# A linear-attention layer with a rational feed-forward on one core: a new order table for the same tasks

## The chip, the cores and the metric

The kernel runs on one core of one Trainium2 chip. The metric is the device time of one execution in microseconds (us). The engines are named as in the profile: PE is TensorE (matmuls; PEld its weight loads), DVE is VectorE, ACT is ScalarE, POOL is GpSimd, SP is SyncE, which only issues transfers here.

## The reference

Two layers follow one another. The first is a linear attention with a decay `w` and a bonus `u` for each head; the second is a feed-forward layer whose activation is a quotient of polynomials. The batch is 4, with 8 heads, 768 positions and 48 elements a head, so the feed-forward sees 3072 rows of 384.

```
for t in range(S):
    cur = einsum('bhd,bhe->bhde', u * k[t], v[t])
    y[t] = einsum('bhd,bhde->bhe', r[t], state + cur)
    state = w * state + einsum('bhd,bhe->bhde', k[t], v[t])
x = y as (3072, 384)
h = x @ w_in                                     # 384 -> 2048
P = a[0] + a[1]*h + a[2]*h**2 + a[3]*h**3
Q = 1 + abs(b[0])*abs(h) + abs(b[1])*h**2
out = (P / (Q + 1e-6)) @ w_out                   # 2048 -> 384
```

## The kernel before

**The attention** works on 24 blocks of 128 positions, two to a token tile of 256. A task of the order table is written as a name, the block or slice, a letter for the engine (P TensorE, D VectorE, A ScalarE, G GpSimd, S SyncE) and a named place for its result. For block n: `Lr`, `Lk`, `Lv` load r, k and v, `LV` brings v into the operand of `y` (a load, or a copy of 64x192 on a compute engine); `sr` and `sk` scale r and k with powers of w; `ba`, `bb`, `bs`, `bv` make the bonus (product, product with u, sum, product with v); `tr` and `tk` transpose r and k on TensorE and `tre`, `tke` copy the result out of its bank; `a` multiplies r and k in tiles of 64x64, `ae` masks it; `kv` makes the change of the state, `kve` adds it and `ca` scales the state; `y` is the output of the block, `ye` adds the bonus; `x` transposes y, `xh` and `xl` store it as a high and a low part (an fp32 number as two).

**The feed-forward** works on 12 token tiles. The 2048 hidden columns are 16 pieces of 128, and a slice s is (as a rule) four of them for one token tile; there are 50 slices. `f1.s.j` makes 128 hidden columns with 9 matmuls of 128x256 (three chunks of the 384, each high by high, high by low, low by high). Its result is in one of two `h` buffers of PSUM. On the slice's 128x1024 elements follow `z`, `q`, `t`, `ln`, `ex` on ScalarE and `u3`, `hi`, `p`, `d`, `lo` on VectorE. `hi` and `lo` are the two parts of the activation; `lo` is the last to read `h` and so frees the buffer for `f1` of slice s+2. `f2.s.half` multiplies them by `w_out`, 12 matmuls of 128x384 for each half of the tokens. `os` brings the sums of a visit to SBUF or adds them there, `od` issues the transfer of the output.

**The weights** come as 28 pieces that are loaded (`cl`) and turned into two fp32 parts by `c0`, `cu`, `ch` on ScalarE, `c2`, `c3` on VectorE and `cr`, `co` on GpSimd (`co` now and then on VectorE). They are spread over the first 150 us. At the very start `pow` makes the powers of w by a scan, `inv` their reciprocals, `sq` is a chain of small instructions on roots of the coefficients, and `turn`, `tab` and `wp` bring the powers into their places over TensorE.

`warm.n` issues n filler matmuls of ones with ones, whose results nobody reads. They only keep TensorE at work while it has nothing else.

**What sets the order.** The table `ORDER` is a string of tasks and is worked off under a manual schedule: each engine's instructions stand in its queue in the order in which the table names its tasks, and wait there for what they need. Nothing is decided at run time. The table was written by a planner outside of the kernel. Buffers are of two kinds: places that the table names (`ta`, `pa`, `h`, `m`), and pools that go around in a fixed turn (`os` with 6 buffers, `dt` with 2, `ldv` with 3, `xt` with 3).

Of the kernel before, what the change touches and what calls it, by code (L numbers as in the profile page):

```python
# [52 lines left out]
tr.0Ppa1 tab.1A c3.6D Lk.1S tre.0.1A warm.8P wpPpa0 tre.0.0A sr.1G warm.2P tr.1Ph1 tre.1.0A tre.1.1A cl.2S Lv.0S sk.2D ba.2Dm0
bb.2D bs.2D sk.0G warm.12P tk.0Ph0 ba.0Gm1 bb.0G kv.2Ppa1 cl.5S sk.1D bv.2D tke.0A a.0Ph1 ba.1Gm2 c0.2A kve.2.1A w128A kve.2.0A
Lr.3S ae.0.0D c2.2Dpa0 Lv.1S cu.2A pad.2G ae.0.1D bb.1G warm.3P kv.0Ph0 Lk.3S kve.0.1A cr.6Gta0 cl.12S tk.1Ppa1 tke.1A bs.0D bv.0G
c3.2D cr.2Gta1 kve.0.0A cl.1S warm.38P kv.1Ph1 c0.5A cu.5A LV.0.1.0A sk.3G sr.3G c2.5Dpa1 ba.3Gm3 bb.3G bs.1D bv.1G LV.0.0.1D
c3.5D LV.0.1.1A a.1Ppa0 ae.1.0D tk.2Ph0 ae.1.1D LV.0.0.0A y.0Ppa1 warm.3P tr.2Ppa0 kve.1.1A c0.12A kve.1.0A c2.12Dh1 ye.0D cl.0S
cl.26S tke.2A c0.1A c2.1Dh0 tre.2.0A Lr.4S Lk.5S ca.0.0G cl.4S warm.10P kv.3Ppa1 tre.2.1A Lk.4S cu.12A c3.12D warm.4P x.0Ph1 ch.2A
a.2Ppa0 Lv.4S xh.0A bs.3D kve.3.0A c3.1D y.1Ph0 kve.3.1A c0.26A xl.0D tr.3Ppa1 cr.12Gta2 cu.1A ae.2.0D ch.12A ae.2.1D warm.6P
y.2Ppa0 tre.3.0A c2.26Dh1 Lv.5S ye.1D x.1Ph0 c0.0A c3.26D warm.1P tk.3Ph1 sr.4G ca.0.1G tre.3.1A xh.1A cl.3S tke.3A ye.2D warm.3P  # L60
x.2Ppa1 xh.2A cu.0A c2.0Dpa0 co.12G xl.1D c3.0D ca.1.0G cr.1Gta3 ch.1A warm.12P a.3Ph1 sk.5D ca.1.1G ae.3.0D tr.4Ph0 cu.26A sk.4G
ba.4Gm1 warm.5P kv.4Ppa0 cl.11S cr.0Gta4 tre.4.0A c0.4A tre.4.1A warm.12P kv.5Ph0 xl.2D co.2G c0.3A cl.9S ae.3.1D cu.3A cl.20S
Lr.5S cu.4A c2.4Dpa1 ch.6A tk.4Ph1 tke.4A kve.4.0D kve.4.1D c3.4D kve.5.1D ch.0A bv.3D c2.3Dpa0 warm.17P a.4Ppa1 tk.5Ph1 co.1D
cu.9A cu.11A c0.11A cr.5Gta5 cl.15S c3.3D cu.20A cl.10S cl.14S kve.5.0D c0.9A warm.15P y.3Ppa0 co.0G f1.0.0Ph0 f1.0.1P tke.5A
# [20 lines left out]
bb.8G cr.17Gta0 ch.17A co.17G f1.7.2P cu.18A cr.18Gta3 LV.4.1.1S os.4.0D LV.4.1.0S bs.7D bv.7G u3.6D ln.6A ex.6A kve.7.0D kve.7.1D
c0.24A f2.5.0P f2.5.1P c2.19Dpa0 c3.19D hi.6Dta0 p.6D tk.8Ppa1 cu.19A cr.19Gta1 tke.8A cu.24A ch.19A co.19G y.6Ppa0 ye.6D tr.8Ppa1
ch.18A f1.7.3P tre.8.1A y.7Ppa0 ca.7.1G tre.8.0A a.8Ppa1 z.7Ata2 d.6D lo.6Dta1 ca.5.0G sk.9G f1.8.0Ph0 t.7Ata5 ye.7D x.6Ppa0 q.7A
co.18G ae.8.0D u3.7D ae.8.1D f1.8.1P f1.8.2P f1.8.3P os.5.0D sr.9G LV.4.0.0S xh.6A xl.6D ln.7A ex.7A os.5.1D f2.6.0P x.7Ppa1
ch.27A cu.25A cr.25Gta6 ch.25A c2.24Dpa0 c3.24D Lk.10S hi.7Dta3 p.7D tr.9Ppa0 tre.9.1A f2.6.1P ca.6.0G xh.7A ca.7.0G co.25G d.7D
tre.9.0A xl.7D kv.8Ppa0 Lk.11S z.8Ata0 lo.7Dta1 kv.9Ppa1 kve.9.0D kve.9.1D cr.24Gta6 ch.24A t.8Ata2 u3.8D f1.9.0Ph1 f1.9.1P  # L90
kve.8.0D sk.10G ba.10Gm2 bb.10G q.8A ln.8A ex.8A co.27D tk.9Ppa1 tke.9A ba.9Gm0 f1.9.2P f1.9.3P z.9Ata5 kve.8.1D bs.8D co.24G
f2.7.0P hi.8Dta4 ca.6.1G Lk.12S sk.12G a.9Ppa1 y.8Ppa0 Lv.10S p.8D d.8D lo.8Dta6 bb.9G bv.8G t.9Ata0 u3.9D Lr.12S f2.7.1P os.7.1D
# [4 lines left out]
f1.11.0Ph1 f1.11.1P os.9.1D ae.10.1D x.9Ph0 xh.9A xl.9D ae.10.0D f1.11.2P kve.10.0D sr.12G os.9.0D ca.9.1G f1.11.3P f1.12.0Ph0
t.11Ata0 f1.12.1P z.11Ata2 q.11A kv.11Ppa1 bs.10D bv.10G Lv.13S kve.10.1D f1.12.2P ba.12Gm1 u3.11D ln.11A bb.12G kve.11.0D
kve.11.1D kv.12Ppa0 kve.12.0D kve.12.1D ba.13Gm0 y.10Ppa1 ye.10D ca.10.1G f2.10.0P tk.11Ppa0 f1.12.3P ex.11A hi.11Dta1 p.11D
bv.11G tke.11A x.10Ppa1 xh.10A tr.12Ppa0 Lr.15S f2.10.1P LV.6.1.1S tre.12.1A d.11D lo.11Dta5 bb.13D tre.12.0A a.11Ppa0 ae.11.1D  # L100
# [847 lines left out]
```

## Time and profile before

| What | us |
|---|---|
| measured time, median of 3 runs (least to greatest) | 559.26 (558.97 to 560.12) |
| span of the profiled execution, first to last instruction | 556.7 |
| PE busy | 544.2 (98%), 5857 matmuls |
| PEld busy | 525.4 (94%) |
| DVE busy | 464.1 (83%), 564 instructions |
| ACT busy | 387.6 (70%), 502 instructions |
| POOL busy | 185.6 (33%), 215 instructions |

The measured time is that of the whole execution; the span is what the profile covers of one. Busy time counts filler matmuls as work, and the shares are means over stretches that differ.

### The profile page before, as it was taken

Reading aid. Unit: us, or ns where it says so; the run is one execution under the profiler, and the core shown is the slowest. Engines: PE = TensorE matmul, PEld = TensorE weight load, DVE = VectorE, ACT = ScalarE, POOL = GpSimd, SP = SyncE. Lnnn points to the kernel's source line nnn. Section 1 sums busy time; section 2 is a strip of 40 time slices with the busy share of each in tenths; the row PEclk is TensorE's granted clock in tenths of the full one; section 3 lists DMA queues with packets and bytes.
Section 4 is the critical chain, followed back from the end, with each engine's and each line's share of the span. In section 5 each row is a group of like instructions: output and inputs, shape, how many; then the busy total and the mean of one; then the engine's idle time right before and its main releaser. Section 6 shows DMA issues by size and latency. Waiting matters only on the chain.

```text
span 556.7 us, 13698 instructions
## 1 busy us (share of the span) xinstructions
PE 544.2 (98%) x5857; PEld 525.4 (94%) x5857; DVE 464.1 (83%) x564; ACT 387.6 (70%) x502; POOL 185.6 (33%) x215
## 2 busy tenths in 40 slices
...
GB/s 147 231 258 269 292 75 86 45 51 1 74 44 44 62 59 125 15 52 101 65 31 2 79 1 29 0 22 44 9 72 1 1 29 1 15 15 1 13 19 34
DMA packets 96857, 34.99 MB, mean 63 GB/s; under 512 B 90130, under 2 KB 93204, under 8 KB 96788
## 3 DMA queue, kind: packets, MB, share of 16 engines
...
q14 instruction: 21, 0.17, 0.1%
q10 hardware_dynamic: 144, 0.20, 0.1%
...
## 4 chain that ended last, share of the span: by engine, by line
PE 64%; DVE 16%; ACT 8%; issue 3%; POOL 2%; DVEq 0%; ACTq 0%; POOLq 0%
PE h L644 26%; PE o L648 8%; PE o L650 8%; PE o L649 8%; DVE q L711 4%; PE y L600 4%; DVE g L707 3%; PE a L550 3%; DVE h L715 3%; DVE h L702 3%; ACT z L694 2%; ACT z L698 2%; PE kv L572 2%; PE tk L527 1%; DVE l L720 1%
## 5 line engine op out<-in xcount | busy, mean ns | idle before, releaser
L644 PE MATMUL h<-xthi,wi 128*128 128x256 f32 x1152 | 218.7, 283 | 1.2 <-DVE l L720 1.1
L644 PEld LDWEIGHTS h<-xthi,wi 128*128 128x128 f32 x1152 | 180.9, 188 | 3.7 <-PE o L650 1.2
L644 PE MATMUL h<-xtlo,wi 128*128 128x256 f32 x576 | 160.8, 279 | 0.0
L648 PE MATMUL o<-wo,g 128*128 128x384 f32 x384 | 132.3, 344 | 0.0
L649 PE MATMUL o<-wo,g 128*128 128x384 f32 x384 | 129.1, 336 | 0.0
L650 PE MATMUL o<-wo,l 128*128 128x384 f32 x376 | 126.5, 337 | 0.0
L644 PEld LDWEIGHTS h<-xtlo,wi 128*128 128x128 f32 x576 | 108.3, 188 | 0.0
L707 DVE SCALAR_TENSOR_TENSOR g<-h,sig,z 128x1024 fp32r<-128x1024 f32 x47 | 60.3, 1283 | 45.3 <-ACT z L698 44.7
L690 ACT ACTIVATE z<-h,off,root 128x1024 f32<-128x1024 f32 x47 | 56.7, 1206 | 46.3 <-PE h L644 40.2
L681 ACT ACTIVATE q<-h 128x1024 f32<-128x1024 f32 (+2 forms) x50 | 49.4, 991 | 34.3 <-PE h L644 30.7
L648 PEld LDWEIGHTS o<-wo,g 128*128 128x128 f32 x384 | 72.2, 188 | 0.6
L649 PEld LDWEIGHTS o<-wo,g 128*128 128x128 f32 x384 | 72.3, 188 | 0.0
L650 PEld LDWEIGHTS o<-wo,l 128*128 128x128 f32 x376 | 70.7, 188 | 0.0
L694 ACT ACTIVATE z<-q,sig 128x1024 f32<-128x1024 f32 x47 | 54.1, 1152 | 22.6 <-DVE h L702 21.4
L711 DVE SCALAR_TENSOR_TENSOR q<-q,sig,g 128x1024 f32<-128x1024 f32 (+2 forms) x50 | 68.0, 1360 | 1.6
L702 DVE SCALAR_TENSOR_TENSOR h<-z,sig,h 128x1024 f32<-128x1024 f32 x47 | 60.3, 1284 | 7.1 <-ACT q L681 4.2
L715 DVE SCALAR_TENSOR_TENSOR h<-h,sig,q 128x1024 f32<-128x1024 f32 (+2 forms) x50 | 62.4, 1248 | 1.5
L685 ACT ACTIVATE q<-q,off,root 128x1024 f32<-128x1024 f32 (+2 forms) x50 | 60.3, 1209 | 0.8
L720 DVE TENSOR_TENSOR l<-h,z 128x1024 fp32r<-128x1024 f32 x47 | 57.4, 1222 | 2.2
L698 ACT ACTIVATE z<-z 128x1024 f32<-128x1024 f32 x47 | 49.9, 1061 | 1.5
L500 POOL TENSOR_TENSOR kh<-kh,wkn 128x384 f32<-128x384 f32 x21 | 23.1, 1103 | 77.5 <-DMA kh<-in_k_dram 77.3
L508 POOL TENSOR_TENSOR m<-rh,kh 128x384 f32<-128x384 f32 x20 | 21.7, 1086 | 53.7 <-PE x L619 52.6
...
## 6 DMA issues: line engine op xcount, KB each, us to landing
...
```

What stands on the lines that cost most here:

```text
L644: nc.tensor.matmul(o, wi_of(j, cc, part), x_[:, cc], start=(n == 0), stop=(n == 3 * NCC - 1))
L648: nc.tensor.matmul(o, hi, wo_of(j, HI), start=first, stop=False)
L649: nc.tensor.matmul(o, hi, wo_of(j, LO), start=False, stop=False)
L650: nc.tensor.matmul(o, lo, wo_of(j, HI), start=False, stop=last)
L685: nc.scalar.activation(g["q"], g["q"], AF.Square, scale=RB, bias=KB)
L694: nc.scalar.activation(g["z"], g["q"], AF.Ln, bias=QE)
L698: nc.scalar.activation(g["z"], g["z"], AF.Exp, scale=-1.0)
L702: nc.vector.scalar_tensor_tensor(g["h"], g["t"], KAP, g["h"], op0=ALU.add, op1=ALU.mult)
L707: nc.vector.scalar_tensor_tensor(g["hi"], g["h"], c0, g["z"], op0=ALU.add, op1=ALU.mult)
L711: nc.vector.scalar_tensor_tensor(g["q"], g["q"], qe, g["hi"].bitcast(F32), op0=ALU.add, op1=ALU.mult)
L715: nc.vector.scalar_tensor_tensor(g["h"], g["h"], c0, g["q"], op0=ALU.add, op1=ALU.subtract)
L720: nc.vector.tensor_mul(g["lo"], g["h"], g["z"])
```

## The change

The 1834 tasks of the old table are 1824 in the new one; those of the computation are the same, and only fillers leave (380 matmuls in 30 entries become 215 in 21). Their order is new, and some tasks stand on another engine: more of `os`, `tre` and `xh` on VectorE instead of ScalarE, `sk`, `ba`, `bv`, `sr`, `co`, `ca` and `kve` differently spread over VectorE, ScalarE and GpSimd. Of the 24 transfers of the output ScalarE issues 15, before one. `os`, `dt`, `ldv` and `xt` get named places like the others. The two halves of `f2` may now stand in either order, and `pw` and `pk` get their buffers at different times.

```
@@ the table, its first and last lines
-CAP = {'m': 4, 'os': 6, 'xt': 3, 'ta': 7, 'pa': 2, 'h': 2, 'ldv': 3}
+CAP = {'m': 4, 'os': 6, 'xt': 3, 'ta': 7, 'pa': 2, 'h': 2, 'ldv': 3, 'dt': 2}
...
-coefS wS cl_D betaA plG st0.1G Lv.2S idG uwS sqD Lv.3S pad.0G Lr.0S st0.0G ctrA pow.0D st0.2A warm.65P turn.0.0Ppa0 pow.1D cl.6S
...
+d.48D p.49D lo.48D d.49D lo.49D f2.48.1P f2.49.1P os.49.1Aos5 od.11.1S f2.48.0P f2.49.0P os.49.0Aos2 od.11.0A
@@ places: one line for each kind
-            tab["pw"] = at.tile([P, NCC, P + 1], F32, tag="os", name="pw", bufs=NO)
-            tab["pk"] = at.tile([P, NCC, P], F32, tag="os", name="pk", bufs=NO)
+            tab["pw"] = at.tile([P, NCC, P + 1], F32, tag=here[0], name="pw")
...
-            t, src = ld.tile([P, H, D], F32, tag="ldv", name=f"vn{n}"), v
+            t, src = ld.tile([P, H, D], F32, tag=here[0], name=f"vn{n}"), v
...
-        d["dt"] = at.tile([P, H], F32, tag="dt", name=f"dt{n}", bufs=2)
+        d["dt"] = at.tile([P, H], F32, tag=here[0], name=f"dt{n}")
```

**The opening on VectorE.** `wcol` is w by columns, `pw` and `pk` its powers and their reciprocals, `half`, `root`, `sig`, `off` belong to the chain of roots. Before, the chain stands ahead of the scan (the row with SCALAR_TENSOR_TENSOR and x3):

```order
L303 TENSOR_SCALAR wcol_84<-wraw_83 128x3
L265 TENSOR_SCALAR rx_98<-cabs_100 128x2
L268 MEMSET lnb_88 128x1
...
L274 RECIPROCAL half_97<-root_96 128x2
...
L288 TENSOR_SCALAR sig_102<-half_97 128x1
L313 COPY pw_173<-cen_90 128x3
L314 SCALAR_TENSOR_TENSOR pw_173<-wcol_84,cen_90,zero_132 128x128 x3
L320 RECIPROCAL pk_174<-pw_173 128x128 x3
```

In the new order of the same place the scan comes right behind `wcol`:

```order
L241 MEMSET ones_81 1x128
L459 MEMSET vs0_105 64x3x192 x2
L303 TENSOR_SCALAR wcol_84<-wraw_83 128x3
L312 COPY pw_147<-cen_90 128x3
L313 SCALAR_TENSOR_TENSOR pw_147<-wcol_84,cen_90,zero_127 128x128 x3
L321 RECIPROCAL pk_167<-pw_147 128x128 x2
L324 RECIPROCAL sq_89<-cen_90 128x3
L325 TENSOR_TENSOR wl_91<-pw_147,sq_89 128x3
L321 RECIPROCAL pk_167<-pw_147 128x128
L265 TENSOR_SCALAR rx_98<-cabs_100 128x2
```

The chain of roots moved behind the scans and the reciprocals.

**The block matmuls on TensorE, around slice 13.** `a13` and `kv14` are the tasks `a.13` and `kv.14`, `y12` and `y13` outputs of blocks. Before, `kv.14` stands by itself between the second half of `f2.12` and `f1.15` (each row repeats; one of each kind is shown):

```order
L650 MATMUL o12_1_3305<-wo_3_925,l12_3167 128x384
L572 MATMUL kv14_3371<-vn14_3268,kh2_112 48x48
L573 MATMUL kv14_3371<-vn14_3268,kh2_112 48x48
...
L644 MATMUL h15_3388<-xthi3_2311,wi_3_0_2025 128x256
L644 MATMUL h15_3388<-xtlo3_2312,wi_3_0_2025 128x256
```

Now it stands behind `a.13`, with `y.12` and `y.13` right behind it:

```order
L645 MATMUL h13_2977<-xthi3_2181,wi_1_2_1307 128x256
L551 MATMUL a13_3031<-ysa1_116,kt_113 64x64
L552 MATMUL a13_3031<-ysb1_117,kt_113 64x64
...
L573 MATMUL kv14_3051<-vn14_2862,kh2_112 48x48
L574 MATMUL kv14_3051<-vn14_2862,kh2_112 48x48
...
L601 MATMUL y12_3070<-vs0_105,ysa0_114 64x48 x2
...
L601 MATMUL y13_3099<-vs0_105,ysa1_116 64x48 x2
```

The four tasks of the blocks have moved together, between `f1.13` and `f1.14`.

**VectorE between `lo.12` and `lo.13`.** The rows with `l12` and `l13` are the two `lo`, `h13`, `g13` and `q13` belong to slice 13. Before:

```order
L720 TENSOR_TENSOR l12_3167<-h12_2831,z12_3027 128x1024
L771 SCALAR_TENSOR_TENSOR os2_1_1881<-o10_1_2935,sig_102,os2_1_1881 128x384
L561 TENSOR_TENSOR ysb1_117<-a13_3192,mask_82 64x512
...
L702 SCALAR_TENSOR_TENSOR h13_3135<-z13_3220,sig_102,h13_3135 128x1024
L561 TENSOR_TENSOR ysa1_116<-a13_3192,mask_82 64x512
L605 TENSOR_TENSOR m12_2887<-y12_3251,m12_2887 128x384
L707 SCALAR_TENSOR_TENSOR g13_3301<-h13_3135,sig_102,z13_3220 128x1024
...
L720 TENSOR_TENSOR l13_3351<-h13_3135,z13_3220 128x1024
```

Now:

```order
L721 TENSOR_TENSOR l12_3025<-h12_2770,z12_2885 128x1024
...
L588 TENSOR_TENSOR vs1_106<-kv14_3051,vs1_106 48x2x192 x2
...
L703 SCALAR_TENSOR_TENSOR h13_2977<-z13_3088,sig_102,h13_2977 128x1024
L505 TENSOR_TENSOR rh1_109<-rh1_109,wrn_92 128x8x48
L606 TENSOR_TENSOR m13_2829<-y13_3099,m13_2829 128x384
L505 TENSOR_TENSOR rh0_107<-rh0_107,wrn_92 128x8x48
L612 TENSOR_TENSOR vs0_105<-vs0_105,w128_94 48x192
...
L424 COPY kt_113<-tk14_3169 128x512
L721 TENSOR_TENSOR l13_3177<-h13_2977,z13_3088 128x1024
```

`kve.14` (two rows of one), two `sr`, two `ca` (one is shown) and `tke.14` have come in between the two `lo`; these stood on VectorE later, or on another engine.

## Rows read from the trace of the kernel before

**Rows 1.** Span and mean granted clock of the core.

```profile
core 0: 556.7 us, clock 1.000
```

**Rows 2.** Stretches: length, then busy PE, PEld, DVE, ACT, POOL; clock, DMA share, GB/s.

```profile
4.46:63.80 59.34, 57.73 (x1042) 53.20 (x1040) 55.70 (x106) 53.84 (x109) 50.18 (x61) 1.00 1.04 249
63.80:152.70 88.90, 86.67 (x927) 83.53 (x925) 85.35 (x99) 74.02 (x102) 69.39 (x69) 1.00 0.32 72
152.70:216.10 63.40, 63.40 (x798) 60.62 (x797) 56.61 (x74) 38.18 (x47) 22.58 (x28) 1.00 0.33 65
216.10:300.00 83.90, 83.90 (x964) 80.24 (x964) 67.59 (x79) 54.21 (x65) 21.36 (x26) 1.00 0.24 50
300.00:550.80 250.80, 249.81 (x2114) 245.41 (x2113) 198.18 (x209) 165.28 (x180) 18.56 (x20) 1.00 0.08 20
```

**Rows 3.** Timeline: `lo.8` on VectorE, first matmul of `f1.10` (start, duration).

```profile
151.44 1.23 DVE L720 TENSOR_TENSOR l<-h,z 128x1024 fp32r<-128x1024 f32 x1
...
153.89 0.28 PE L644 MATMUL h<-xthi,wi 128*128 128x256 f32 x1
```

**Rows 4.** Timeline: `lo.13` on VectorE, first matmul of `f1.15`.

```profile
214.87 1.23 DVE L720 TENSOR_TENSOR l<-h,z 128x1024 fp32r<-128x1024 f32 x1
...
217.86 0.39 PE L644 MATMUL h<-xthi,wi 128*128 128x256 f32 x1
```

**Rows 5.** Timeline of TensorE, opening; idle time before an instruction in brackets.

```profile
2.07 6.04 PE L808 MATMUL idle_bank<-wones 128*128 128x128 bf16 x65 [2.07 <-POOL wones L242]
9.34 0.33 PE L345 MATMUL ptab<-identw,pw 128*128 128x128 f32 x1 [1.23 <-DVE pw L314]
9.51 0.50 PE L808 MATMUL idle_bank<-wones 128*128 128x128 bf16 x6
9.84 0.28 PE L345 MATMUL ptab<-identw,pw 128*128 128x128 f32 x1
```

**Rows 6.** Timeline of VectorE, opening.

```profile
4.46 0.27 DVE L303 TENSOR_SCALAR wcol<-wraw 128x3 f32<-128x3 f32 x1 [4.46 <-DMA wraw<-in_w_dram]
...
8.81 1.23 DVE L314 TENSOR_TENSOR_SCAN pw<-wcol,cen,zero 128x128 f32<-128x128 f32 x3
```

**Rows 7.** Timeline of TensorE: `f1` into `a`; second half of `kv` into `y`.

```profile
52.41 0.28 PE L644 MATMUL h<-xtlo,wi 128*128 128x256 f32 x1
52.53 0.28 PE L644 MATMUL h<-xthi,wi 128*128 128x256 f32 x1
52.73 0.27 PE L550 MATMUL a<-ysa,kt 64*64 64x64 f32 x1
...
181.38 0.21 PE L573 MATMUL kv<-vn,kh 128*48 128x48 f32 x1
181.42 0.29 PE L600 MATMUL y<-vs,ysa 128*64 128x48 f32 x4
```

**Rows 8.** VectorE groups by shape, whole span: busy, mean ns, idle before.

```profile
L561 DVE TENSOR_TENSOR ysa<-a,mask 64x512 f32<-64x512 f32 x24 | 16.7, 695 | 2.2 <-PE a L551 1.5
L633 DVE TENSOR_TENSOR xtlo<-x,xthi 128x384 fp32r<-128x384 f32 x24 | 13.2, 552 | 3.8 <-ACT xthi L423 3.7
L423 DVE COPY vs<-vn 64x192 f32<-64x192 f32 x16 | 4.0, 282 | 0.4 <-DMA vn<-in_v_dram 0.2
L500 DVE TENSOR_TENSOR kh<-kh,wkn 128x384 f32<-128x384 f32 x3 | 2.3, 768 | 0.0
L611 DVE TENSOR_TENSOR vs<-vs,w 48x192 f32<-48x192 f32 x5 | 2.0, 396 | 0.1
L420 DVE TENSOR_TENSOR wi<-bwi,wi 128x512 fp32r<-128x512 f32 x1 | 1.7, 1691 | 0.0
L769 DVE TENSOR_SCALAR os<-o,sig 128x384 f32<-128x384 f32 x2 | 1.2, 612 | 1.1 <-PE o L650 1.1
```

**Rows 9.** Timeline of VectorE: `p` of two slices.

```profile
137.05 2.59 DVE L711 SCALAR_TENSOR_TENSOR q<-q,sig,g 128x1024 f32<-128x1024 f32 x1
...
148.72 1.28 DVE L711 SCALAR_TENSOR_TENSOR q<-q,sig,g 128x1024 f32<-128x1024 f32 x1
```

More of the change, by code (lines that the diff above doesn't have):

```diff
@@ L53 @@
[L53 to L64, printed above, removed]
@@ L85 @@
[L85 to L92, printed above, removed]
@@ L97 @@
[L97 to L100, printed above, removed]
@@ L165 @@
-os.49.0A od.11.0A os.49.1D od.11.1S
+pad.0G pad.2G st0.0G plGos0 st0.1D uwSos1os2 ubG wS cl_D ctrA pow.0Dos3 turn.0.0Ph0 ubpPpa0 pad.1G st0.3G st0.2A pow.1D pow.2D
+warm.4P turn.1.0P inv.2Dos4 inv.0D turn.2.0P wlD warm.22P turn.0.1Ph1 turn.2.1P inv.1D warm.5P wpPpa1 turn.1.1P Lv.2Sldv0 coefS
+Lv.3Sldv1 LV.1.0.0A Lk.2S tab.0A LV.1.1.1A Lr.0S sr.0G tr.0Ph0 betaA sqD ubeA LV.1.1.0A mskG Lr.2S sr.2G tab.1A tre.0.1A LV.1.0.1A
+Lk.0S cl.6S c0.6A w128A tre.0.0A sk.2G ba.2Dm0 warm.24P kv.2Ph1 sk.0G tk.0Ppa0 kve.2.0A tke.0A kve.2.1A Lr.1S sr.1D bb.2D bs.2Ddt0
@@ new lines @@
+c2.6Dpa1 warm.8P tr.1Ph0 cl.2S Lv.0Sldv2 tre.1.1A tre.1.0A c0.2A cu.2A c3.6D warm.5P a.0Ph1 ae.0.1D ae.0.0D c2.2Dh0 ba.0Gm1 bb.0G
+bs.0Ddt1 bv.2G Lk.1S kv.0Ppa0 kve.0.1A cl.5S kve.0.0A c0.5A c3.2D c2.5Dpa1 sk.1G warm.13P tk.1Ph1 tke.1A warm.15P a.1Ppa0 cu.6A
+Lr.3S Lv.1Sldv0 kv.1Ph1 LV.0.1.0A LV.0.1.1A LV.0.0.0A LV.0.0.1D warm.12P y.0Ph0 ba.1Gm2 bb.1G bs.1Ddt0 ae.1.1D c3.5D ae.1.0D cl.0S
+c0.0A c2.0Dpa1 bv.0G ye.0D c3.0D cl.12S kve.1.1A c0.12A c2.12Dh0 kve.1.0A tr.2Ppa0 tre.2.1D tre.2.0A sr.3G bv.1G cr.2Gta0 Lk.3S
@@ new lines @@
+sk.3G cr.6Gta1 ca.0.0G ch.2A co.2G c3.12D warm.6P tk.2Ph1 tke.2A y.1Ppa1 ye.1D cl.1S c0.1A c2.1Dpa0 c3.1D ch.6A tr.3Ph1 tre.3.1A
+warm.4P x.0Ppa1 xh.0Axt0 xl.0D a.2Ph0 ae.2.0D ae.2.1D cu.1A tre.3.0A ba.3Gm3 Lk.4S sk.4G bb.3G tk.3Ppa0 x.1Ppa1 xh.1D cl.26S cl.4S
+c0.4A tke.3A c0.26A c2.4Dpa0 xl.1D kv.3Ph1 cu.0A kve.3.0A kve.3.1A y.2Ph0 Lr.4S sr.4G warm.8P tr.4Ppa1 ca.1.0G ca.0.1G cr.1Gta2
+bs.3Ddt1 ye.2D c2.26Dh1 c3.4D Lv.4Sldv2 Lv.5Sldv0 cu.4A tre.4.0A cu.12A tre.4.1A c3.26D a.3Ph0 ae.3.0D ae.3.1D x.2Ppa0 cl.3S cu.3A
@@ new lines @@
+xh.2Axt1 xl.2D tk.4Ph1 c0.3A kv.4Ppa1 kve.4.0D c2.3Dpa0 bv.3G ca.1.1G ch.1A tke.4A y.3Ph0 ye.3D c3.3D kve.4.1D warm.4P a.4Ph1
+ae.4.1D ae.4.0D cl.9S cu.9A c0.9A cr.0Gta3 ch.0A Lk.5S sk.5G tk.5Ph0 cu.26A cl.10S cl.20S c0.20A tke.5A kv.5Ppa0 kve.5.0D x.3Ppa1
+co.1G co.0G f1.0.0Ph0 f1.0.1P f1.0.2P c0.10A xh.3A cu.20A cl.14S cu.14A c2.20Dh1 c3.20D xl.3D kve.5.1D c0.14A c2.14Dpa1 c2.10Dh1
+ba.4Gm1 Lr.5S bb.4G sr.5G cr.3Gta4 ba.5Gm2 cu.5A cr.5Gta5 cl.15S c0.15A cu.15A tr.5Ppa0 tre.5.1A tre.5.0D cl.11S c0.11A f1.0.3P
@@ new lines @@
+q.2A co.8G cr.7Gta5 co.9G cr.11Gta2 ch.7A co.7G u3.2D ln.2A warm.13P tr.7Ppa0 tre.7.1A c3.16D c2.17Dh1 c2.18Dpa1 c3.17D c3.18D
+c2.13Dpa1 ex.2A hi.2Dta3 p.2D d.2D c3.13D lo.2Dta5 warm.10P f2.1.1P f2.1.0P os.1.0Dos0 sk.6G c0.21A c0.23A c2.21Dpa1 cr.12Gta0
+ch.12A tre.7.0A ch.11A cu.13A cr.26Gta6 ch.26A cu.21A ba.6Gm0 co.11G co.26G f1.3.0Ph1 f1.3.1P f1.3.2P tk.6Ppa0 tke.6A f1.3.3P
+z.3Ata1 t.3Ata2 u3.3D q.3A co.12G cr.10Gta6 ch.10A cr.14Gta4 warm.5P kv.6Ppa0 kve.6.1D c3.21D kve.6.0D c2.23Dpa1 ln.3A ex.3A
@@ new lines @@
+kv.8Ppa1 ca.5.1G cr.24Gta4 ch.24A kv.9Ppa0 kve.9.0D kve.9.1D co.24G sr.11G ca.6.0G kve.8.1D kve.8.0D q.8A ln.8A ex.8A hi.8Dta6
+p.8D d.8D lo.8Dta2 cr.25Gta4 ch.25A co.25G ca.7.0G f1.9.0Ph1 f1.9.1P tk.9Ppa0 f1.9.2P f1.9.3P tr.9Ppa1 tke.9A z.9Ata4 tre.9.0A
+tre.9.1A t.9Ata1 f2.7.1P ba.9Dm2 q.9A u3.9D ln.9A sk.10G a.9Ppa0 ae.9.1D bs.8Ddt0 ae.9.0D os.7.1D f1.10.0Ph0 f1.10.1P f1.10.2P
+ex.9A hi.9Dta0 p.9D f2.7.0P d.9D os.7.0D lo.9Dta3 bb.9G bs.9Ddt1 f1.10.3P z.10Ata5 q.10A f2.8.1P Lk.11S t.10Ata4 u3.10D ln.10A
@@ new lines @@
+ex.10A bv.8D bv.9D Lr.10S sr.10G LV.4.0.1S y.8Ppa1 ye.8D y.9Ppa0 ye.9D ba.10Gm0 bb.10G bs.10Ddt0 tr.11Ph1 f2.8.0P tk.10Ppa1
+tr.10Ppa0 tre.11.0A tke.10A tre.11.1A hi.10Dta1 sk.11G ba.11Gm3 Lr.12S sr.12G tre.10.0D p.10D d.10D ca.7.1D bv.10D bb.11D f2.9.0P
+lo.10Dta2 os.9.0D Lv.11Sldv0 LV.5.1.0S Lr.13S LV.5.0.0A Lk.12S Lv.13Sldv2 Lr.14S LV.5.0.1S x.8Ppa1 tre.10.1A xh.8Axt1 f1.11.0Ph1
+f1.11.1P f1.11.2P x.9Ppa0 xh.9A LV.5.1.1A xl.9D xl.8D f1.11.3P a.10Ph0 ae.10.1D sk.12G kv.10Ppa0 kve.10.0D t.11Ata6 z.11Ata5
@@ new lines @@
+Lr.15S y.11Ph1 ye.11D z.12Ata3 t.12Ata5 tke.12A u3.12D q.12A ln.12A ex.12A a.12Ppa1 ae.12.1D kv.13Ppa0 kve.13.0D kve.13.1D
+f2.11.1P hi.12Dta6 os.11.1D tk.13Ph1 tr.13Ppa0 tre.13.0A od.2.1S tre.13.1A tke.13A Lk.15S LV.7.1.1S LV.6.1.1S f2.11.0P x.10Ppa0
+f1.13.0Ph1 f1.13.1P f1.13.2P f1.13.3P p.12D ae.12.0D bs.13Ddt1 d.12D sk.15G ba.14Gm0 bb.14G bv.13G ca.10.0G lo.12Dta1 xh.10Axt2
+xl.10D a.13Ppa1 ae.13.1D ae.13.0D LV.6.1.0S kv.14Ppa0 kve.14.0D kve.14.1D y.12Ph0 ye.12D t.13Ata2 z.13Ata0 u3.13D q.13A ln.13A
@@ new lines @@
+f1.17.3P z.17Ata2 os.15.0Aos4 lo.16Dta3 f2.15.1P tr.16Ppa0 t.17Ata1 q.17A kve.16.1D ca.14.0D u3.17D ln.17A ex.17A os.15.1Dos0
+Lv.17Sldv1 sr.18D ca.12.0D kve.16.0D f1.18.0Ph0 f1.18.1P f2.16.0P tre.16.0A LV.8.1.1A f1.18.2P tk.16Ppa1 tke.16A f1.18.3P
+tre.16.1D Lk.18S sk.18G bv.15G hi.17Dta0 p.17D d.17D Lr.19S y.15Ppa0 ye.15D lo.17Dta4 Lv.18Sldv2 od.1.1A z.18Ata5 t.18Ata2 q.18A
+u3.18D ln.18A ex.18A a.16Ppa1 ae.16.1D kv.17Ppa0 kve.17.1D kve.17.0D hi.18Dta1 Lv.19Sldv0 LV.8.1.0S LV.8.0.0S LV.9.1.1S od.0.0S
```

215 lines of the change are left out of this document (104 added, 111 removed).

## Prediction

> **What bounds the kernel now.** I read the span and the clock first: one core, 556.7 us, no stretch below full clock [rows 1]. The table of stretches comes next, because the share of TensorE (98% over the span) hides that the limits change. I cut the span where the last elementwise step of a slice, `lo`, ends: `lo.0` at 63.8, `lo.8` at 152.7, `lo.13` at 216.1 us. Up to 63.8 us VectorE is busy 55.70 of 59.34 us and up to 152.7 us 85.35 of 88.90, so 96% in the second stretch; TensorE is as full there, but not with its own work: the filler matmuls of `warm` sit in these two stretches. From 152.7 us on TensorE is busy 63.40 of 63.40 and 83.90 of 83.90 us, while VectorE falls to 89%, 81% and 79% [rows 2]. So there are two regimes. Until about slice 8 to 13, VectorE sets the pace and TensorE's fillers cover its waits; after that every us of TensorE work counts, and VectorE has 7, 16 and 53 us spare in the three stretches.
>
> The handover is the `h` buffer. There are two, `f1` of slice s+2 needs the one that `lo` of slice s frees. `lo.8` starts at 151.44 and takes 1.23, it ends at 152.67; the first matmul of `f1.10` stands at 153.89 [rows 3], so it is 1.22 us behind its release. `lo.13` ends at 216.10, `f1.15` starts at 217.86 [rows 4].
>
> **TensorE's part of the change.** (a) Opening. Today 65 fillers run from 2.07 us, and the first real transpose stands at 9.34 because it waits for the scan of the powers of w [rows 5]. On VectorE `wcol` is there at 4.46+0.27, but the scan starts at 8.81: the chain of small root instructions stands between [rows 6]. The new order puts the scan right behind `wcol`: with 0.41 for the first scan (a third of 1.23) that is 5.2 us, and the copy of a column and the semaphores between the engines come on top. I take 6.0 for the transpose, 3.3 us earlier; the bounds are 5.2 and, if the root instructions slip in front again, 9.3. (b) Fillers. Behind that transpose 315 of 380 fillers ran, now 215 do. Six of them took 9.51 to 9.84, 0.055 us each [rows 5]: 100 x 0.056 = 5.6 us. (c) Array shapes. `a` (64x64 tiles) and the first half of `kv` use 64 rows, the rest 128. Inside `f1` one matmul follows the other by 0.12 (52.41 to 52.53), the first of `a` by 0.20 (52.73): a change of shape costs about 0.09. From the second half of `kv` to `y` it costs nothing (0.04, 181.38 to 181.42) [rows 7]. Counted in the two tables, switches fall from 127 to 82, since `a` and `kv` now stand together 16 times, against never: 45 x 0.09 = 4.1 us; `a` to `kv` itself isn't in the trace, at a full switch the gain falls by 16 x 0.09 = 1.4, at none it is the 4.1 that I use. (d) Transposes are followed by `f1` or `f2` rather than by fillers a few times more often, 0.6 us. Together 13.6 us: that is what TensorE alone could give, if nothing kept it waiting.
>
> **VectorE's part** decides how much of this is seen, and VectorE has more to do, not less: many evictions (`os`, `tre`, `xh`) come to it from ScalarE. I count what stands ahead of the two marks. The opening gives it little: the same root instructions follow the scan.
> Ahead of `lo.8` nine instructions leave: the weight piece `co.1` (1.69), `sk.1`, `sk.2`, `sk.5` (2.3 together), `os.0.1` (0.61), and `bs.8`, `bv.2`, `bv.3`, `co.27` (0.55 each, the row of a 128x384 operation), 6.8 us. Seven come: `bv.6`, `sr.1`, `xh.1`, `xh.4` (0.55 each), `os.1.0` (0.61), `tre.2.1`, `tre.5.0`, 4.2 us [rows 8]. A `tre` on VectorE isn't in the trace. The nearest rows are a copy of 64x192 (0.28) and a 64x512 operation out of the same kind of bank (0.695); it has 64x512, so I take 0.69, with 0.28 the sum is 0.8 lower, and there is no row that makes it dearer. So `lo.8` comes 2.6 - 0.1 = 2.5 us earlier, at 150.2, if VectorE waits as long as before (3.55 us of 88.90). Released at once, `f1.10` starts near 150.35, 3.5 us earlier than 153.89. Behind that point TensorE has 3.3 us more (`f2.7.0` and `y.8` now stand behind it), 36 of the 45 saved switches (-3.3), and 0.5 of (d) less: -0.5. By this mark the end moves by -4.0 us.
> Ahead of `lo.13` 11 instructions of 7.2 us leave: eight of those nine (not `bs.8`), `LV.5.0.0` and `bb.13`. 22 come, 12.3 us: four `tre` (2.8), five `ca` (0.40 each), `bv` three times, `sr` three times, `xh` and `kve` twice each (0.55 each), and `ba.9`, `tke.14`, `os.1.0` (0.6 to 0.7 each) [rows 8]; instructions that don't depend on each other overlap by some 0.08, so 4.2 us more, not 5.1. VectorE idles 6.8 us of the 63.40 between the marks [rows 2]; the largest of it are waits for `a`, `kv` and `y` of a TensorE that is full, and these shrink when TensorE is ahead. With all of them kept, `lo.13` ends at 220.3; with none, at 213.5. Behind `f1.15` TensorE has 2.7 us less (24 switches, `tk.14`, `tr.14` and `x.11` moved ahead, `kv.15` moved behind). That gives the end 220.45 - 217.86 - 2.7 = -0.1 and 213.65 - 217.86 - 2.7 = -6.9. The middle is -3.5, near the -4.0 of the first mark. I take **-3.5 us**.
>
> **At no cost:** the named slots change which buffer a tile gets, not how many there are; the loads of rh, kh and vn stand early enough that TensorE, full from 152.7 on, hides them. 14 more output transfers are issued from ScalarE's queue; ScalarE is busy 165.28 of 250.80 us at the end [rows 2], an issue there delays by itself nothing that TensorE waits for; without that cover each would add its issue time ahead of a `z`. The last matmuls, evictions and transfer follow one another as before.
>
> [...] One `p` of VectorE took 2.59 us, another, of the same shape, 1.28 [rows 9]: something beside it doubles the first. [...]
>
> **The rivals.**
> *VectorE doesn't pace.* Its waits vanish and TensorE takes all of 13.6 us: 559.26 - 13.6 = 545.7. For it: TensorE's fillers show slack in its own queue. Against it: 96% of VectorE in the second stretch, and 2.5 us less work can't bring 13.6.
> *The change gives nothing.* VectorE's 4.2 us more ahead of `lo.13` find it with its 6.8 us of waits intact: -0.1, so 559.2. For it: the waits are for other engines' answers, whose latency stays. Against it: the longest name TensorE, which is earlier.
> [...]
>
> **How the numbers follow.** The measured median is 559.26, the profiled span 556.7, so 2.56 us lie around it; the sums are differences and go onto the median: 559.26 - 3.5 = **555.8**. Chances: VectorE paces 0.56 (its own range 552.4 to 559, from -6.9 and -0.1); TensorE alone 0.12; nothing 0.16; slower 0.16. A run of this kernel tells apart 0.2%, or 1.1 us: 558.1 to 560.4 is "same". From the first case 0.53 and the second 0.12 are faster, 0.65; same 0.18, made of the third and the edge of the first; slower 0.17. The range 548 to 562 leaves out most of the second case and the far half of the fourth.
>
> **What would show it.** Right: first transpose near 6 us, `lo.8` ending near 150, `f1.10` within 0.3 us of it, `lo.13` between 213 and 220, VectorE at 95% up to there, and TensorE without waits from about 215 us on, with some 2.5 us less work behind. Wrong: `lo.8` no earlier while VectorE waits more than 4 us in the second stretch (then waits replaced work), `tre` on VectorE far from 0.69, switches at another price than 0.09, or a granted clock below 1.00 in the first 150 us.

## The result, and the profile after

The changed kernel takes 564.93 us (564.30 to 565.80), the kernel before 559.15 in the same comparison: ratio 1.0108, 95% interval [1.0095, 1.0121], 5.8 to 6 us slower. Forecast were 555.8 us, in a range from 548 to 562. The ratio of new_tail, below, leaves out one of its ten executions, which took 2924.43 us for a reason that isn't known. The profiled execution took 564.30 us, with a span of 562.6.

The page of the kernel after, busy time by engine, has TensorE at 539.6 us, 4.6 less than before, in a span that is 5.9 longer:

```profile
PE 539.6 (96%) x5692; PEld 521.1 (93%) x5692; DVE 479.6 (85%) x594; ACT 374.9 (67%) x480; POOL 178.1 (32%) x199
```

So TensorE idles 10.5 us more. The stretches, cut at the same marks as in [rows 2] (end of `lo.0`, `lo.8`, `lo.13`), show where: `lo.8` came early, `lo.13` late, and TensorE isn't full behind it.

```profile
4.38:64.72 60.34, 55.69 (x933) 49.75 (x933) 55.16 (x102) 50.85 (x101) 47.50 (x58) 1.00 1.02 245
64.72:150.31 85.59, 83.85 (x852) 80.50 (x850) 83.61 (x100) 73.56 (x104) 67.98 (x66) 1.00 0.31 70
150.31:220.09 69.78, 67.14 (x850) 64.33 (x848) 65.02 (x88) 37.00 (x45) 27.51 (x28) 1.00 0.34 62
220.09:300.00 79.91, 79.06 (x839) 77.14 (x840) 68.76 (x82) 49.33 (x56) 12.51 (x13) 1.00 0.16 33
300.00:556.92 256.92, 253.49 (x2224) 249.35 (x2223) 205.60 (x225) 161.83 (x173) 19.09 (x20) 1.00 0.11 27
```

Between `lo.8` and the last matmul TensorE was idle 0.99 us before (398.1 us of the last three rows, less their busy time). Now it is idle 2.64 + 0.85 + 3.43 = 6.9 us. The two handovers, for [rows 3, 4], in the timeline of the kernel after:

```profile
149.09 1.22 DVE L721 TENSOR_TENSOR l<-h,z 128x1024 fp32r<-128x1024 f32 x1
...
150.37 0.39 PE L645 MATMUL h<-xthi,wi 128*128 128x256 f32 x1
...
218.88 1.22 DVE L721 TENSOR_TENSOR l<-h,z 128x1024 fp32r<-128x1024 f32 x1
...
220.15 0.39 PE L645 MATMUL h<-xthi,wi 128*128 128x256 f32 x1
```

`f1.10` starts at 150.37 (forecast: 150.35). `f1.15` starts at 220.15, 2.3 us later than before; the forecast had 213.65 to 220.45, and took the middle. The last matmul starts at 556.92, 6.1 later than before.

The waits of TensorE in the kernel after (us in total, times, longest) name new ones:

```profile
PE ptab L346 <- DVE pw L313: 5.4, 1, 5.4
PE h L645 <- DVE l L721: 2.6, 5, 0.8
PE o L651 <- DVE g L721: 2.2, 1, 2.2
PE tr L528 <- ACT kt L424: 1.8, 1, 1.8
PE o L649 <- DVE os L772: 1.6, 1, 1.6
PE kv L573 <- DVE m L606: 1.1, 2, 0.7
```

In the kernel before the same list has, behind the two waits of the opening, only two above half a us:

```profile
PE o L808 <- DVE os L769: 1.2, 1, 1.2
PE h L644 <- DVE l L720: 1.1, 2, 0.9
```

The 1.6 us stand in front of `f2.10.1`, and are part of the late `f1.15`. VectorE is late with `os.9.1` there, because of the line ahead of it in the timeline:

```profile
183.40 1.29 DVE L716 SCALAR_TENSOR_TENSOR h<-h,sig,q 128x1024 f32<-128x1024 f32 x1
184.72 2.65 DVE L424 COPY vs<-vn 64x192 f32<-64x192 f32 x2
184.78 0.56 POOL L612 TENSOR_TENSOR vs<-vs,w 48x192 f32<-48x192 f32 x1
185.30 1.01 POOL L505 TENSOR_TENSOR rh<-rh,wrn 128x384 f32<-128x384 f32 x1
186.28 0.98 POOL L514 TENSOR_TENSOR m<-m,ub 128x384 f32<-128x384 f32 x1
187.39 0.62 DVE L772 SCALAR_TENSOR_TENSOR os<-o,sig,os 128x384 f32<-128x384 f32 x1
187.93 0.41 DVE L424 COPY vs<-vn 64x192 f32<-64x192 f32 x2
188.06 0.44 PE L649 MATMUL o<-wo,g 128*128 128x384 f32 x1 [1.55 <-DVE os L772]
```

Two copies (`LV.6.0.0`) take 2.65 us, the next pair of the same shape (`LV.6.0.1`) 0.41. The long pair ends at 187.37, 0.1 us behind the last of three GpSimd instructions that stand without a gap beside it.

The 2.2 us stand in `f2.47`: VectorE does `hi.48`, `p.48` and the two small checks of the flag ahead of `lo.47` (the L721 with 128x512), and `f2.47.0` waits for it:

```profile
551.11 0.48 DVE L708 SCALAR_TENSOR_TENSOR g<-h,sig,q 128x256 fp32r<-128x256 f32 x1
551.62 0.48 DVE L712 SCALAR_TENSOR_TENSOR q<-q,sig,g 128x256 f32<-128x256 f32 x1
552.02 0.27 DVE L375 TENSOR_REDUCE oks<-flagt 1x1 f32<-1x128 f32 x1
552.33 0.14 DVE L376 CAST okf<-oks 1x1 int32<-1x1 f32 x1
552.40 0.67 DVE L721 TENSOR_TENSOR g<-h,q 128x512 fp32r<-128x512 f32 x1
553.00 0.46 DVE L708 SCALAR_TENSOR_TENSOR g<-h,sig,q 128x256 fp32r<-128x256 f32 x1
...
553.12 0.44 PE L651 MATMUL o<-wo,g 128*128 128x384 f32 x1 [2.24 <-DVE g L721]
```

The waits don't make the whole. The other part is a pace: the matmuls of `f1` and `f2` follow each other more slowly **from the first to the last**. Taken from the starts in the trace (mean over all pairs within a task; steps above 150 and 210 ns left out), `f1` has 116.9 ns a matmul before and 118.7 after, `f2` 173.8 and 175.8. One half of an `f2`, first and last of 12 matmuls, takes 1.90 us from start to start before:

```profile
538.17 0.34 PE L648 MATMUL o<-wo,g 128*128 128x384 f32 x1
...
540.07 0.34 PE L650 MATMUL o<-wo,l 128*128 128x384 f32 x1
```

In the kernel after it takes 1.94:

```profile
541.90 0.33 PE L649 MATMUL o<-wo,g 128*128 128x384 f32 x1
...
543.84 0.34 PE L651 MATMUL o<-wo,l 128*128 128x384 f32 x1
```

1728 matmuls of `f1` and 1152 of `f2` times 1.9 and 2.0 ns are 5.6 us. Small matmuls don't show it: `y` has 29.4 ns before and 29.3 after, the fillers 56.1 and 56.5.

### The profile page after: what moved, and what is told of

Same layout as the page of the kernel before. It is cut to its first block, busy times and chain, and to the rows that moved or that the text cites. A ratio compares the mean times of both kernels' runs of the same rounds, so it can differ in the third digit from the quotient of the medians.

```text
span 562.6 us, 13321 instructions
## 1 busy us (share of the span) xinstructions
PE 539.6 (96%) x5692; PEld 521.1 (93%) x5692; DVE 479.6 (85%) x594; ACT 374.9 (67%) x480; POOL 178.1 (32%) x199
## 4 chain that ended last, share of the span: by engine, by line
PE 52%; DVE 20%; ACT 5%; issue 3%; DMA 1%; POOL 1%; SPq 0%; ACTq 0%; DVEq 0%; POOLq 0%
PE h L645 22%; PE o L649 8%; PE o L651 8%; PE o L650 7%; DVE q L712 3%; DVE g L708 3%; DVE l L721 3%; DVE h L716 3%; DVE h L703 2%; PE a L551 2%; ACT z L695 1%; PE y L601 1%; PE kv L573 1%; ACT z L699 1%; PE x L620 1%
## 5 line engine op out<-in xcount | busy, mean ns | idle before, releaser
L645 PE MATMUL h<-xthi,wi 128*128 128x256 f32 x1152 | 222.1, 286 | 2.9 <-DVE l L721 2.6
L695 ACT ACTIVATE z<-q,sig 128x1024 f32<-128x1024 f32 x47 | 54.2, 1152 | 25.2 <-DVE h L703 23.5
L712 DVE SCALAR_TENSOR_TENSOR q<-q,sig,g 128x1024 f32<-128x1024 f32 (+2 forms) x50 | 64.8, 1296 | 1.6
L721 DVE TENSOR_TENSOR l<-h,z 128x1024 fp32r<-128x1024 f32 x47 | 57.4, 1222 | 1.9
L514 POOL TENSOR_TENSOR m<-m,ub 128x384 f32<-128x384 f32 x21 | 21.6, 1030 | 62.5 <-DVE m L509 44.6
```

What stands on the lines that cost most here:

```text
L645: nc.tensor.matmul(o, wi_of(j, cc, part), x_[:, cc], start=(n == 0), stop=(n == 3 * NCC - 1))
L695: nc.scalar.activation(g["z"], g["q"], AF.Ln, bias=QE)
L712: nc.vector.scalar_tensor_tensor(g["q"], g["q"], qe, g["hi"].bitcast(F32), op0=ALU.add, op1=ALU.mult)
L721: nc.vector.tensor_mul(g["lo"], g["h"], g["z"])
```

## The experiments

**What makes the pace: the starts in SBUF?** The change gives `os`, `xt`, `ta` and the others new places. In the kernel before `xt` and `ta` begin at multiples of 64 bytes, in the one after 32 bytes off. (These starts are those of the build; the trace doesn't hold them.) The shift can be worked out from the two kernels: before, all six buffers of `os` are as large as the largest tile in them, `pw` (3x129 numbers, 1548 bytes a partition, the next 1536), and with named places only one is. In the two builds the starts of neighbouring `os` buffers lie 1568 bytes apart before, and after it 1536, but for the one that holds `pw`: 5 x 32 = 160 bytes less. The first four runs shift places with an unused tile and leave the order alone:

```
@@ new_pad32; old_pad32 the same in the old kernel
             tab["pw"] = at.tile([P, NCC, P + 1], F32, tag=here[0], name="pw")
+            at.tile([P, 8], F32, tag="pad", name="pad")
@@ old_all64; new_all64 with the pad above too
+    cst.tile([P, 8], F32, name="pad0")
     vs2 = [cst.tile([P, 5, 2, NP, D], F32, name=f"vs{i}") for i in range(B // 2)]
...
         hsum = cst.tile([HD, 2], F32, name="hsum")
+        cst.tile([P, 24], F32, name="pad1")
```

> The changed kernel with one unused tile of 32 bytes a partition, so that the places xt and ta begin at multiples of 64 bytes again, as before the change. Theory A (start address): the matmuls of f1 and f2 follow each other by 116.9 and 173.8 ns again instead of 118.7 and 175.8, and 1728 and 1144 of them give back 5.6 us: about 559.3. Rival B (the slower pace comes with the new order, or with the execution that was profiled): pace and time stay, 564.9.

> The kernel before, in its old order, with one unused tile of 32 bytes that moves xt and ta off the multiples of 64 bytes. Theory A: pace 118.7 and 175.8 ns, 559.2 + 5.6 = 564.8. Rival B: 559.2, since the order is the old one.

> The kernel before with the weights too at multiples of 64 bytes (they begin 32 bytes off in both kernels). If each operand's start counts by itself, f1 gains at its weight side and f2 at its moving side some 2 ns a matmul more: 559.2 - 5.6 = 553.6. If only xt and ta count: 559.2. Rival B: 559.2.

> The changed kernel with xt, ta and the weights at multiples of 64 bytes. If each operand's start counts by itself: 564.9 - 11.2 = 553.7. If only xt and ta count: 559.3. Rival B: 564.9.

Measured: new_pad32 1.0128 [1.0098, 1.0158], old_pad32 1.0036 [1.0025, 1.0048], old_all64 1.0071 [1.0050, 1.0092], new_all64 1.0122 [1.0094, 1.0150], all against the kernel before. Theory A falls: no version at multiples of 64 got its pace back, and old_all64 is slower by 4 us. Rival B falls too: 32 unused bytes made the old order 2 us slower. Set side by side, the six profiles gave another rule, theory C: what counts is the **distance of the two operands**, start of the moving one minus start of the stationary one (the one of the weight load), in bytes of a partition, modulo 256 (`xt` minus `wi` in `f1`, `wo` minus `ta` in `f2`). Within a kernel it is the same for all matmuls of a kind, which fits that no slice stood out in these profiles. At the distance 128, the kernel after and old_all64 had the same pace (118.7 and 175.8 to 175.9) in different orders and at different starts (`xt` and `ta` at 224 and 0, weights at 96 and 128, modulo 256). old_all64 also prices that pace by itself: nothing but places differs from the kernel before, and it costs 4 of the 5.8 us.

**Four more distances, and the old ones under the new order.**

```
@@ new_dist, next to pw
+            at.tile([P, 40], F32, tag="pad", name="pad")
@@ old_d192_64; old_d96_32 with [P, 16] and old_d224_160 with [P, 48]
+            at.tile([P, 40], F32, tag="pad", name="pad")
@@ old_d96_32 and old_d224_160, between xt and ta
+            ew.tile([P, 32], F32, tag="pad", name="padt")
```

> The changed kernel with 160 unused bytes ahead of xt and ta, so that the distance of the two SBUF operands' starts, moving minus stationary, modulo 256, is 32 in f1 and 224 in f2, as in the kernel before (the change made both 128). Theory C (that distance sets the pace; the six profiles so far give the same pace wherever the distance is the same): 116.9 and 173.8 ns, and of 1728 x 1.9 + 1144 x 2.0 = 5.6 us the part behind the stretch that VectorE paces, some 4 us, comes back: 560 to 561. Rival D (each program gets a pace of its own, by no rule): any pace from 116.9 to 119.5 and 173.8 to 176.6, time within 563 to 567.

> The kernel before with the distances 96 in f1 and 32 in f2. Theory C: f1 between its neighbours at 64 and 128, 117.8 to 118.8 ns; f2 near that at 0, 174 ns; time within 2 us of before. Rival D: no order among the distances.

> The kernel before with the distances 192 in f1 and 64 in f2. Theory C: f1 between 160 and 0, 117.8 to 119.5 ns; f2 between 0 and 96, 174 to 176.6 ns; some 2 to 4 us slower than before. Rival D: no order among the distances.

> The kernel before with the distances 224 in f1 and 160 in f2. Theory C: f1 117.8 to 119.5 ns, f2 near its neighbours at 128 and 192, 175.7 ns; some 3 us slower than before. Rival D: no order among the distances.

new_dist has 116.9 and 173.8 ns, as theory C says (its starts modulo 256 are those of the kernel before too, so it tells against rival D, not which of distance and starts counts), and 1.0055 [1.0033, 1.0078]: 561.45 us, 3 us back of the 6. The same half of `f2` in it, 1.92 us:

```profile
539.70 0.34 PE L650 MATMUL o<-wo,g 128*128 128x384 f32 x1
...
541.62 0.34 PE L652 MATMUL o<-wo,l 128*128 128x384 f32 x1
```

One execution each gave 563.52 us (96, 32), 557.13 (192, 64) and 560.62 (224, 160), against 558.61; the second was expected slower than before, not faster. All paces by distance, the mean of one profile or more, in ns:

| distance | 0 | 32 | 64 | 96 | 128 | 160 | 192 | 224 |
|---|---|---|---|---|---|---|---|---|
| `f1` | 119.5 | 116.9 | 117.8 | 119.8 | 118.7 | 117.8 | 115.7 | 118.3 |
| `f2` | 173.9 | 175.2 | 173.3 | 176.6 | 175.9 | 173.9 | 175.5 | 173.8 |

My guesses for the unmeasured ones, between the neighbours, were right for 224 in `f1` alone: the pace isn't smooth in the distance.

**The best distances alone, the waits, the opening.** old_best is old_d192_64 again, timed in more rounds. The other three start from new_dist:

```
@@ new_tail, a part of the last slices
-u3.48D u3.49D ex.47A hi.47Dta0 p.47D d.47D q.48A q.49A ln.48A ex.48A hi.48Dta3 p.48D f2.46.0P f2.46.1P flagmD lo.47D f2.47.0P
+ex.47A hi.47Dta0 z.48Ata6 z.49A t.48A od.10.0S p.47D t.49A u3.48D d.47D u3.49D q.48A lo.47D q.49A ln.48A ex.48A hi.48Dta3 p.48D
@@ new_lv
-LV.6.0.0D os.9.1D LV.6.0.1D
+LV.6.0.0A os.9.1D LV.6.0.1A
@@ new_fill
+warm.28P turn.0.0Ph0
```

> new_dist (561.45) with the last slices' elementwise tasks in the order of the kernel before: lo.47 ahead of hi.48 and p.48 on VectorE, ex.47 ahead of the others on ScalarE. If the wait of 2.4 us in f2.47 and the slower matmuls behind it come from that order: about 558.5. Rival: the wait moves to f2.48 and f2.49, whose inputs then come later, and 561.4 stays.

> new_dist with the two copies LV.6.0.0 and LV.6.0.1 on ScalarE instead of VectorE. If a copy from SBUF to SBUF on VectorE stands still while GpSimd works (2.67 us for two that take 0.41 elsewhere) and so holds back os.9.1: the wait of 1.64 us in front of f2.10.1 goes, 559.8 to 560.5. Rival: os.9.1 is late for another reason, or the gain is lost at the next wait: 561.4.

> new_dist with 28 filler matmuls ahead of the first transpose. If TensorE's slow first 11 us of real work (to some 16.3 us) cost the end something, 1 to 3 us come back: 558.5 to 560.5. If VectorE paces there, as predicted: the same, 561.4, with f1.10 still at 150.4.

> The kernel before with the distances 192 in f1 and 64 in f2, timed (one look gave 557.13). By the pace, 1.1 ns less for 1728 matmuls and 0.46 for 1144, of which some 3/4 lie behind the stretch that VectorE paces: 1.8 us faster, 556.9. Rival (the single time was chance): 558.6.

old_best: 0.9965 [0.9951, 0.9978], 2.0 us faster than the kernel before, by places alone. It is the only version here that beats both kernels beyond doubt. Its half of `f2` takes 1.91 us, and `f1` is at 115.7 ns.

new_tail: 1.0009 [0.9999, 1.0020], 2.6 us better than new_dist; the wait in `f2.47` is gone, and 0.2 is left in the list of TensorE's waits from 540 us on:

```profile
PE o L654 <- DVE g L724: 0.2, 1, 0.2
```

new_lv: 1.0051 [1.0036, 1.0067], not distinguishable from new_dist by its time. Its trace shows the wait undone: `f2.10.1` follows `f1.12.3` at once, `os.9.1` (L775) stands right behind `d.11`. But now the next VectorE instruction, a `ca`, takes 2.21 us instead of 0.35, from 185.15 to 187.36; in new_dist the three GpSimd instructions beside the copies stand from 185.41 to 187.90:

```profile
184.51 0.61 DVE L775 SCALAR_TENSOR_TENSOR os<-o,sig,os 128x384 f32<-128x384 f32 x1
185.15 2.21 DVE L615 TENSOR_TENSOR vs<-vs,w 48x192 f32<-48x192 f32 x1
...
186.08 0.27 PE L648 MATMUL h<-xthi,wi 128*128 128x256 f32 x1
186.19 0.34 PE L652 MATMUL o<-wo,g 128*128 128x384 f32 x1
```

That fits GpSimd's work as the cause: the long instruction is what VectorE happens to do there, not the copy as such. No run moved GpSimd's work, so it isn't shown by itself. Nor does all that stands beside a train of GpSimd instructions wait for its end: in the kernel after a `ca` at 193.50 us took 0.71, while GpSimd worked without a gap from 192.22 to 195.08. From `f1.10` to `f1.15` it is 68.9 us in new_lv, 69.9 in new_dist and 70.2 in new_tail, so the wait undone is worth 1.0 to 1.3 us; the times, whose interval is wider than that, didn't show it.

new_fill: 1.0074 [1.0056, 1.0093], no gain; `f1.10` starts at 152.12, 1.1 us later than in new_dist. The slow steps of 0.107 us end at 12.7 us instead of 15.8, but the fillers also push the first transpose from 5.36 to 6.86. So this trade doesn't pay; what an earlier end of the slow steps would bring without it is not shown.

**All together.** new_fix has the distances of before, the old tail and `LV.6.0` on ScalarE; new_fix_192 has other starts with the distances 192 and 64; new_fix_warm puts fillers into TensorE's waits of the opening.

```
@@ new_fix_192 against new_fix
-            at.tile([P, 40], F32, tag="pad", name="pad")
+            at.tile([P, 56], F32, tag="pad", name="pad")
+    cst.tile([P, 8], F32, name="pad0")
+        cst.tile([P, 24], F32, name="pad1")
@@ new_fix_warm against new_fix
+warm.8P tr.2Ppa0
+warm.5P y.1P
+warm.26P tr.3P
```

> The changed kernel with the operand distances of before (32 and 224), the old order of the last slices and LV.6.0 on ScalarE: new_dist, new_tail and new_lv in one. If distance and these two waits are what the forecast missed, and the two waits add up: 0.2% or 0.3% below the kernel before, 557 to 558. Rival (something else in the new order still costs what the forecast left out, or the waits don't add up): 559 or more.

> The same with the distances 192 and 64, at other absolute starts than in old_best (weights at 128 instead of 96, xt and ta at 64 instead of 32, modulo 256). Theory C: 115.7 and 173.3 ns, and 1.5 to 2 us less than new_fix, 555 to 556.5. Rival (the absolute starts count too): any other pace.

> new_fix with 39 filler matmuls where TensorE waits at 27 to 33 us (8 ahead of tr.2, 5 ahead of y.1, 26 ahead of tr.3). In new_fix the profiled execution falls to the lower clock from 30.1 to 33.5 us, and its times go from 557.0 (mean clock 0.998) to 561.8 (0.992). If falls behind these waits make the spread: no fall there, and nearly all times at 557 to 557.8, 0.3% below the kernel before. Rival (the falls come elsewhere, or cost nothing because VectorE paces there): the same spread, median 558.

new_fix: 0.9995 [0.9978, 1.0013], the kernel before within the measurement. From 1.0108 down to 0.9995 are 6.3 us, so distance and the two waits add up to what was lost, but not to the forecast gain. Its 11 executions lie between 557.0 and 561.8 us, and the mean granted clock goes with them by and large: 0.998 in the four at 557.0 to 557.4, 0.992 to 0.993 in the three above 560. Such falls stand in the profile of new_dist in two stretches, one in the opening behind waits of TensorE, one behind the wait in `f2.47`, both at a granted clock of 0.50. The kernel after has the same waits in the opening (1.8, 0.6 and 0.3 us between 20 and 36 us) and in its profile no fall behind them. The two stretches of new_dist:

```profile
32.90:36.30 3.40, 3.40 (x43) 3.01 (x41) 1.94 (x3) 2.84 (x7) 3.40 (x5) 0.50 0.79 172
551.80:555.20 3.40, 3.40 (x13) 3.40 (x12) 1.61 (x4) 0.00 (x0) 0.00 (x0) 0.50 0.07 17
```

new_fix_192: 0.9987 [0.9972, 1.0001], not told apart from new_fix, where 1.5 to 2 us less were expected, at 116.5 and 173.4 ns. For `f2` the distance foretold the pace (173.3); for `f1` it did not (115.7 in old_best). The mean hides why: at the distance 192 most `f1` tasks go at either about 113 or about 118 ns, in both kernels. Steps of 115 ns or less are 49% in old_best, 48% in old_d192_64 and 31% in new_fix_192. So the mean is a mix, and what picks the pace of a task, absolute starts or order, is not shown. Of the 17 profiles those at equal distance agree within 0.2 ns, except this one: theory C isn't the whole rule.

new_fix_warm: 1.0037 [1.0026, 1.0049], slower than new_fix. In its profile the granted clock was 0.50 all the same, from 17.6 to 24.4 us, behind a wait of 2.3 us for a scaled r, and `kv.5` lost 2.4 us to something that the trace doesn't name. What sets these falls and the length of the opening from execution to execution stays open.

## Why the prediction was wrong, step by step

- **The opening**: the transpose was to come at 6.0 us and stands at 5.36, inside the bounds of 5.2 and 9.3. TensorE's first work ran at a slow pace, and longer than in the kernel before, where fillers at 0.107 us each end at 6.7 us: 24 fillers behind `tr.0` take 2.76 us, and the pace of 0.107 us each ends at about 16 us. At `f1.10` nothing of it is left to see: it starts as forecast, and VectorE paces there.

```profile
5.36 0.45 PE L346 MATMUL ptab<-identw,pw 128*128 128x128 f32 x1 [5.36 <-DVE pw L313]
...
13.62 2.76 PE L809 MATMUL idle_bank<-wones 128*128 128x128 bf16 x24
```

- **VectorE up to `lo.8`**: forecast to end at 150.2, it ended at 150.31, with a `tre` at 0.68 to 0.69. VectorE's work fell by 2.3 us over both stretches (2.5 forecast), and its waits stayed at 7.2 in sum. That the sum stayed is partly luck: there are 1.5 us more in the first stretch and 1.6 less in the second.
- **VectorE up to `lo.13`**: 213.5 to 220.3, taken at the middle, for which no row spoke; it came at 220.09, the upper end. VectorE is busy 8.4 us more between the marks, where 6.7 were counted: the two long copies (2.65 us for 0.41) are 2.2 of it. The overlap of some 0.08 that the count used is there in the kernel before: 201 of 223 overlapping pairs have 0.07 to 0.09. It idles 4.8 us (69.78 less 65.02) of once 6.8, where the middle needed 3.4. The step that failed is "these shrink when TensorE is ahead": the wait for `a` is 1.6 us, before 1.4, and TensorE wasn't ahead but idle for 2.6 us itself. A wait of 0.6 us for a load of r is new; the forecast had it hidden.
- **"At no cost: the named slots"** is the step that failed worst. No transfer and no buffer count changed, as it said; but the new places set another distance between the operands of 2880 matmuls. That was 5.6 us of pace. 3.9 of it lie behind `f1.15` (1188 matmuls of `f1`, 840 of `f2`), and 3 us came back in new_dist, the same within the measurement. Ahead of it VectorE paces, and nothing came back: `f1.10` to `f1.15` takes 69.8 us in the kernel after and 69.9 in new_dist.
- **"TensorE full from 152.7 on"** was carried over from the kernel before as if it belonged to the program and not to its order. 6.9 us of waits stand there now. Undoing the two behind `f1.10` that stand largest in the list brought 2.6 us (new_tail) and, in the trace, 1.0 to 1.3 us (new_lv); in new_fix waits for `lo` and `ye` of less than 1 us each are left, 2.7 us behind `f1.15` against 1.0 before.
- **TensorE's work**: with pace and large waits undone, the way from `f1.15` to the last matmul is 331.97 us in new_fix against 332.95: 1.0 less. The forecast was 2.7 less without waits, and 1.7 us more of waits make the difference. The count of 45 switches holds if `y` and the second half of `kv` are taken as a shape of their own: the two tables then have 150 and 105, by rows alone 96 and 64, and from `f1` into `y` it is 0.21 us as well. The price of a switch (205.06 to 205.27 from `f1` into `a`, 0.09 above a step) and the free step from `a` to `kv` (`kv.14` starts at 206.03, before the last of `a.13` at 206.20) were right. For (d), the next matmul starts 0.028 us behind the last of a transpose's if it is of `f1` or `f2`, and 0.109 if it is a filler (medians); 50 transposes stand ahead of `f1` or `f2` now, 42 before, and 8 x 0.081 is 0.6 us.
- **The single price on VectorE**, as the sums above count it, was kept mostly: `ba`, `bv` and `sr` have means of 549, 591 and 684 ns in the kernel after, and the 47 `p` 1343, 1410 before. What doubled the one `p` of [rows 9] is not shown: in the kernel before GpSimd is at work beside both, without a gap from 135.82 to 141.29 beside the 2.59 us and from 148.84 on beside the 1.28. Two cases paid more than double: the pair of copies took 2.65 us for 0.41, ending 0.1 us behind the last of three GpSimd instructions, and the `ca` of new_lv 2.21 for 0.35; the `ca` of 0.71 us in the kernel after paid double.
- **Slower, and a granted clock below 1.00 in the first 150 us**: the 0.16 for a slower kernel, and with it the upper end of the range, was an estimate; no run shows what a fall of the clock by itself costs. In new_dist the clock fell to 0.50 for 3.4 us twice, behind waits without fillers, and in new_fix the executions above 560 us have a mean of 0.992 to 0.993. But it isn't the main cause. In the profile of the kernel after the clock is 1.00 from 16.5 to 558.0 us, behind the last matmul, and one of its executions had a mean of 1.000 and took 564.41 us.
- **The sum**: at the last matmul -3.5 us were forecast and 6.1 measured, 9.6 apart. `f1.15` stands 3.1 us behind the middle (217.05), and behind it the pace costs 3.9 us and waits 3.3 more (4.28 against 0.99). These are 10.3; what gave 0.7 back is not shown.
